# Five engine queues of an attention and MLP kernel, issued in another written order

## The chip, the cores and the metric

The kernel runs on one core of a Trainium2 chip. The metric is the device time of one execution in microseconds (us); before the change three runs took 714.17, 713.13 and 709.47 us, a median of 713.13.

A core has a matrix engine (TensorE, PE in the profile), a vector engine (DVE), a scalar engine (ScalarE, ACT), GpSimd (POOL), and a sync engine (SP) that here only issues DMAs. Each engine takes its instructions in the order of its own queue and waits at the head of the queue until what that instruction needs is there.

## The reference

Inputs are q, k, v of 4 batches, 8 heads, 768 positions and 64 dimensions in fp32, and the weights of a gated MLP (512 to 1536 to 512) with an RMSNorm gain.

```python
k_sum = k.reshape(B, H, nb, 32, D).max(axis=3)     # 24 block keys
v_sum = v.reshape(B, H, nb, 32, D).mean(axis=3)
scores_l = scale * q @ k.T, kept where |i - j| < 16
scores_s = scale * q @ k_sum.T + log(32)
a = softmax of both together
out = a @ concat(v, v_sum)
x = out, 3072 tokens of 512
xn = x / rms(x) * rms_g
(silu(xn @ w_gate) * (xn @ w_val)) @ w_out
```

## The kernel before, in words

The tokens are cut into 24 units of 128 (batch 0 is units 0 to 5, batch 3 units 18 to 23), and the units into groups for the MLP of 384, 128, 256 and then six times 384 tokens (`GROUPS`, groups 0 to 8). A product in full precision is made of fp16 high and low halves, three matmuls to a product.

The work is a list of some 760 steps (`PLAN`), each a call of one function. The names that the change and the prediction use:

- `su_*` (L889 to L1078): units 0 to 5 in fp32, loaded at the start; `su_vsum` (L961) sums v by blocks on PE, `su_v2` (L1002) and `su_v` (L991) load rows of v.
- `load_gv`, `decode_gv`, `split_gv` (L550 to L590) and `load_o`, `decode_o`, `scale_o`, `row_o`, `conv_o` (L557 to L650): bring the weights in, scale them and split them into halves. `row_o` takes sums of squares on ACT (L627), `scale_o` makes scales of them, and `conv_o` writes the scaled output weights (L649, L650).
- `sum_load`, `sum_fold`, `sum_scale` (L657 to L710): load k and v of batches 1 to 3 by pieces into two buffers (`hn`), fold each to block sums on ACT (L676) and POOL (L682), and scale a half batch with a small matmul (L699).
- `load_unit`, `load_k`, `prep_k`, `prep_q`, `fill_k`, `prep_v` (L744 to L820): load a unit's q, k and v, scale and split them. `prep_k` and `prep_q` each turn their tile with a transposing DMA on SP (L729, L796: `kT`, `qT`).
- `scores u g` (L822): matmuls L834 out of `kT` and `qT`, two to each unit; `expo u g` (L844): exponentials on ACT (L849), the split by ACT and POOL (L431, L436), and a transposing DMA on SP (L858: `eT`); `attend u` (L861): matmuls L875 out of `eT`, and the division on DVE (L879 to L881), which also frees the attention's PSUM banks.
- `norm_a`, `norm_b` (L1079, L1090): RMSNorm and a transposing DMA on SP (L1111: `xT`).
- `gate_val grp f T` (L1245, matmuls L1258) and `project grp f T tok0` (L1282, matmuls L1292): the MLP of a group by 12 slices f of 128 hidden columns.
- `make_t`, `make_s`, `seven`, `swish` (L1141 to L1243): for groups 5 to 8 the gate and value products in a seven-product scheme, matmuls L1190.

What an engine does first is not left to a scheduler. `ORDER` (L149) holds for each of the five queues (PE, Activation, DVE, Pool, SP) a permutation of that queue's instructions, numbered as the steps of `PLAN` make them: each entry is a jump from the last number, and "xN" a run of N consecutive numbers. `in_order` (L334) decodes it and ties every instruction to the one before it on its queue:

```python
for run in runs.split():
    jump, _, count = run.partition("x")
    n += int(jump)
    seq += range(n, n + int(count or 1))
    n = seq[-1] + 1
for a, b in zip(seq, seq[1:]):
    tc.add_manual_dep(traced[e][b], traced[e][a].name, after, reason="order")
```

Of the kernel before, what the change touches and what calls it, by code (L numbers as in the profile page):

```python
# [1339 lines left out]
```

## Time and profile before

| what | us |
|---|---|
| three runs | 714.17, 713.13, 709.47 |
| median | 713.13 |
| the profiled execution | 715.84 |
| its span, first to last instruction | 713.8 |
| PE busy in the span | 676.3 |
| DVE busy | 546.8 |
| ACT busy | 497.0 |
| POOL busy | 221.4 |

Some 2.0 us of the profiled execution lie outside its span. The mean granted clock of TensorE was 0.988 of full speed. "Busy" counts the time in which an engine runs an instruction; the page's matmul times overlap each other, so idle time of PE is what its busy time leaves of a stretch.

### The profile page before, as it was taken

How to read it: one execution, taken by the hardware profiler on the slowest of the kernel's cores; microseconds unless marked ns; L12 is line 12 of the kernel's file. 1: busy time of each engine (PE TensorE's matmuls, PEld its weight loads, DVE VectorE, ACT ScalarE, POOL GpSimd, SP SyncE). 2: the span in 40 equal slices, each digit the busy share in tenths (PEclk: the TensorE clock that was granted, in tenths of full speed). 3: DMA queues.
4: the chain of work that ended last, by engine and by line, in shares of the span. 5: the costliest groups of instructions: out<-in, count | busy, mean ns of one | idle time of the engine just before them, and what ended most of it. 6: DMA issues, size and time to landing. Idle time of an engine off the chain costs nothing.

```text
span 713.8 us, 16151 instructions
## 1 busy us (share of the span) xinstructions
PE 676.3 (95%) x5854; PEld 480.1 (67%) x5854; DVE 546.8 (77%) x1599; ACT 497.0 (70%) x1095; POOL 221.4 (31%) x321
## 2 busy tenths in 40 slices
PE   6898999977999999999999999999999999999997
PEld 4586767963457755565565555787877688878873
DVE  3698988958779957677989789998888778675443
ACT  3597877678997768756876776877788668744433
POOL 5473332550234244512132444232133213310000
PEclk9999999998999999999999999999999999999999
DMA  9999644634688768778569857193759563320001
GB/s 190 290 330 250 207 156 126 125 86 82 119 171 160 154 150 154 153 141 138 134 137 175 134 124 152 29 165 69 146 116 148 116 87 74 65 53 31 16 30 45
DMA packets 243860, 93.33 MB, mean 131 GB/s; under 512 B 227716, under 2 KB 227716, under 8 KB 243780
## 3 DMA queue, kind: packets, MB, share of 16 engines
q1 hardware_dynamic: 239172, 84.78, 57.1%
q10 hardware_dynamic: 3456, 6.29, 2.4%
q0 software_dynamic: 1152, 1.22, 0.8%
q8 instruction: 46, 0.75, 0.5%
q14 instruction: 34, 0.28, 0.1%
HBM read 50.45 MB, written 6.59 MB: 80 GB/s over the span
## 4 chain that ended last, share of the span: by engine, by line
PE 54%; DVE 13%; ACT 11%; DMA 10%; issue 5%; SPq 4%; POOL 2%; ACTq 0%; POOLq 0%; DVEq 0%
PE acc L1292 14%; PE gv L1190 14%; PE gv L1258 14%; PE acc L1258 4%; DMA eT<-ee 3%; SPq L745 3%; DMA qT<-qs 2%; PE att L875 2%; PE att L834 2%; DVE sm L838 2%; ACT sm L849 1%; DMA hn<-in_v_dram 1%; ACT junk L627 1%; DMA xT<-xs 1%; PE att L1026 1%
## 5 line engine op out<-in xcount | busy, mean ns | idle before, releaser
L1292 PE MATMUL acc<-wo,hhl 128*128 128x512 f16 x864 | 232.0, 382 | 4.2 <-ACT wo L649 2.8
L1258 PE MATMUL gv<-xT,w_gv 128*128 128x384 f16 (+2 forms) x1296 | 219.3, 305 | 3.3 <-DVE vv L820 0.9
L1258 PEld LDWEIGHTS <-w_gv 128*128 128x128 f16 x1584 | 141.4, 99 | 75.2 <-issue 5.6
L1292 PEld LDWEIGHTS <-hhl 128*128 128x128 f16 x864 | 81.6, 98 | 66.6 <-issue 5.1
L436 POOL TENSOR_TENSOR ee<-sm,ee 128x256 f16<-128x256 f32 (+1 forms) x72 | 68.0, 961 | 163.6 <-ACT ee L431 149.4
L1190 PEld LDWEIGHTS <-w_gv 128*128 128x128 f16 x1008 | 86.6, 98 | 9.1 <-issue 0.4
L849 ACT ACTIVATE sm<-sm,mx,c 128x192 f32<-128x192 f32 x144 | 70.6, 538 | 1.5
L1190 PE MATMUL gv<-S,w_gv 128*128 128x192 f16 x504 | 63.8, 246 | 0.1
L838 DVE CUSTOM_DVE_ANT_0 sm<-att,mask 128x192 f32<-128x192 f32 x144 | 44.3, 351 | 10.7 <-POOL ee L436 8.0
L1190 PE MATMUL gv<-xT,w_gv 128*128 128x192 f16 x504 | 52.1, 246 | 0.0
L1190 PEld LDWEIGHTS <-wo 128*128 128x128 f16 x540 | 47.0, 98 | 7.1 <-issue 1.9
L1190 PE MATMUL gv<-xT,wo 128*128 128x192 f16 x360 | 48.9, 246 | 1.2 <-DVE xT L1178 0.8
L875 PEld LDWEIGHTS <-eT 128*128 128x128 f16 x720 | 36.2, 97 | 18.2 <-DMA eT<-ee 4.4
L875 PE MATMUL att<-vv,eT 128*128 128x65 f16 x720 | 44.1, 193 | 4.2 <-DMA eT<-ee 3.0
L834 PE MATMUL att<-kT,qT 128*128 128x192 f16 x288 | 41.9, 246 | 4.2 <-DMA qT<-qs 3.0
L436 POOL TENSOR_TENSOR xs<-x,xs 128x512 f16<-128x512 f32 x21 | 25.2, 1202 | 53.4 <-ACT xs L431 48.2
L1258 PE MATMUL acc<-xT,w_gv 128*128 128x384 f16 (+1 forms) x288 | 40.6, 273 | 0.0
L676 ACT ACTIVATE junk<-hn 96x512 uint8<-96x512 f32 x48 | 30.0, 625 | 12.7 <-DMA hn<-in_v_dram 7.4
L1267 ACT ACTIVATE th<-gv,gains 128x384 f32<-128x384 f32 (+1 forms) x42 | 22.8, 544 | 22.9 <-PE gv L1258 15.6
L431 ACT CAST ee<-sm 128x512 f16<-128x512 f32 (+1 forms) x72 | 34.7, 507 | 5.8 <-DMA eT<-ee 4.8
L682 POOL TENSOR_TENSOR hn<-hn 96x512 f32<-96x512 f32 x18 | 22.9, 1271 | 45.6 <-DMA hn<-in_v_dram 27.3
L834 PEld LDWEIGHTS <-qT 128*128 128x128 f16 x288 | 25.8, 98 | 16.6 <-DMA qT<-qs 4.6
(308 smaller groups left out, 1347.2 us busy)
## 6 DMA issues: line engine op xcount, KB each, us to landing
wo<-in_moe_w_gate_dram SPq DMA_DIRECT2D x6, 1024.0 KB
wo<-in_moe_w_val_dram SPq DMA_DIRECT2D x6, 1024.0 KB
wo<-in_moe_w_out_dram SPq DMA_DIRECT2D x6, 1024.0 KB
out_dram<-ob ACTq DMA_DIRECT2D x23, 256.0 KB
hn<-in_k_dram SPq DMA_DIRECT2D x24, 192.0 KB
hn<-in_v_dram SPq DMA_DIRECT2D x24, 192.0 KB
qr_l<-in_q_dram SPq DMA_DIRECT2D x15, 256.0 KB
vr_l<-in_v_dram SPq DMA_DIRECT2D x15, 256.0 KB
```

The lines of the kernel that those rows point to most:

```text
L431: nc.scalar.copy(o, i)
L436: (nc.vector if ENG.get(op, "p") == "v" else nc.gpsimd).tensor_tensor(o, a, b, op=ALU.subtract)
L676: nc.scalar.activation(junk[0:96], y[:, o:o + DM], AF.Square, accum_out=d["ss"][:, j:j + 1])
L682: eng.tensor_tensor(x[:, 0:w], x[:, 0:w], y[:, 0:w], op=op)
L834: nc.tensor.matmul(pt[:, j * SC:(j + 1) * SC], lhsT=s["qT"][:, a * H + h, :], rhs=kT[:, h, :], start=(a == 0), stop=(a == 1))
L838: nc.vector.tensor_tensor_reduce(sm[:, i, :], pt[:, j * SC:(j + 1) * SC], mask, 1.0, NEG, op0=ALU.add, op1=ALU.max, accum_out=mx[:, i:i + 1])
L849: nc.scalar.activation(sm[:, i, :], sm[:, i, :], AF.Exp, scale=s["c"][:, 0:1], bias=mx[:, i:i + 1])
L875: nc.tensor.matmul(po[r][:, h // 2, 0:D + 1], lhsT=e, rhs=vv[:, 0:D + 1], start=(n == 0), stop=(n == len(pairs) - 1))
L1190: nc.tensor.matmul(bank[:, i * T2:(i + 1) * T2], lhsT=right(n, wi, c), rhs=left(xi, c), start=start, stop=(i == 1 and c == 1 and wi == 1), ...
L1258: nc.tensor.matmul(pt[:, 0:T], lhsT=w_gv[:, f - f % 2 + i, wi, c, f % 2, :], rhs=x[:, xi, c, 0:T], start=(n == 0), stop=(n == 3 * NC - 1))
L1267: nc.scalar.activation(th, pg[:, 0:T], AF.Tanh, scale=f_sc[:, f - f % 2:f - f % 2 + 1])
L1292: nc.tensor.matmul(accs[grp][j], lhsT=h[:, js], rhs=wo_hl[f // 2][:, wi, f % 2, :], start=(f == first and n == 0), stop=(f == (first - 1) ...
```

## The change

Only the five strings of `ORDER` are replaced. `PLAN`, the functions, the tiles, the buffers and the number of instructions on each queue (PE 5709, Activation 1003, DVE 1407, Pool 330, SP 382) stay, and each new string is a permutation of the same numbers. So nothing is computed otherwise, and every wait for data stays; what changes is what stands ahead of what on a queue. The first line of the PE and of the SP string, old and new (a leading - is the diff's mark):

```diff
 ORDER = dict(
     PE="""
-0x52 6x4 -10x6 4 1 -2 1 4x6 -10x4 34x3 -28x2 -4 -2 1 4x5 3 -4x3 16x4 1 -32 10 1 18x2 -20x2 -4 -12 14 4 -5x4 1 7 3x2 1
...
+0x22 36x2 -38x18 20 -21x8 13 -14x10 8x4 -7 -2 2 -2 13 4x2 -15x4 1 1 -4 1 27x3 -22 -7x2 5 20x2 1 -2 2x2 -23x2 -6x4 23
...
     SP="""
-1 -2 21 -20 -2 1 13 -14x2 13 -12 9 -5x2 -9 -2 4 -2 9 -8 -5 2 3 8x2 1 27 -27 -2 1x2 1 -11 -3 78 -45 -35 3 7 -3 11 -3 -8
...
+2 17 -21x2 20 -4 -17x2 10 -11x2 4 -4 7 -5 -6 1 4 -5 2 3x2 2 5 -4 7 2 -3 -6 2 -2 -8 2 12 -11 -5 33 -2 -15 3x2 -14 20 -13
...
```

Decoded, the order shows these moves (positions on a queue count from 0; "ahead" and "behind" are seen from the instruction named):

| queue | first instruction of | position | what changed sides |
|---|---|---|---|
| SP | `su_v 2` | 20 to 18 | behind now: 2 loads of `su_v2 0` |
| SP | `load_gv 4` | 25 to 34 | ahead now: 7 loads of `su_v2`, `load_gv 5`, `load_gv 6` |
| SP | `load_gv 11` | 54 to 58 | ahead now: `sum_load 1 0 0 2` and 6 loads of `su_v2`; behind now: 2 of `load_unit 6`, 1 of `su_v2 3` |
| ACT | `decode_gv 4`, its last pass | 49 to 50 | ahead now: a copy of `norm_b 0` |
| ACT | `sum_fold 1 1 1 1` | 141 to 139 | behind now: one pass each of `decode_o 10` and `gate_val 1 5`; `norm_a 5` stays ahead |
| ACT | `conv_o 0` | 170 to 168 | behind now: one pass each of `prep_q 6` and `gate_val 2 1` |
| DVE | `scale_o`, last pieces | | between them no longer: `prep_k 8` |
| PE | `gate_val 3 0` | 1738 to 1741 | ahead now: 3 matmuls of `project 2 10` |
| PE | `scores 10 0` | 1761 to 1762 | ahead now: the same 3; behind now: 2 of `gate_val 3 0` |
| SP | `expo 14 1` | 258 to 257 | behind now: the transposition of `norm_b 12` and a load of `load_unit 16`; ahead now: another load of `load_unit 16` |
| ACT | `expo 14 1` | 519 to 518 | behind now: copies of `make_t 4`, `make_t 5`, a pass of `gate_val 4 7` |
| POOL | `expo 14 1` | 233 to 231 | behind now: 2 DMA issues of `prep_v 14`, a pass of `norm_a 13` |
| PE | `scores 16 1`, second matmul | 2908 to 2974 | ahead now: 31 matmuls of `attend 15`, 24 of `gate_val 5 7`, 11 of `project 4 10` and `4 11` |
| DVE | `attend 15` | | five of its passes now in one run; `make_s 5 0` was between |
| PE | `scores 19 0` | 3697 to 3718 | ahead now: 21 matmuls of `seven 6 1` |
| PE | `scores 20 0` | 3962 to 3971 | ahead now: 7 matmuls of `seven 6 3`, 2 of `project 6 3` |
| PE | `attend 20` | 4200 to 4208 | ahead now: 8 matmuls of `seven 6 5` |
| PE | `scores 22 0` | 4452 to 4476 | ahead now: 24 matmuls of `seven 7 1` |

Everywhere else neighbours change places as well, mostly by a few positions; on SP, whose queue is the shortest, the moves reach farthest in time.

## Rows read from the trace of the kernel before

**Rows 1.** The page's part 1: busy us and share of each engine
```profile
PE 676.3 (95%) x5854; PEld 480.1 (67%) x5854; DVE 546.8 (77%) x1599; ACT 497.0 (70%) x1095; POOL 221.4 (31%) x321
```

**Rows 2.** Windows: length, busy of PE, PEld, DVE, ACT, POOL; clock, DMA share, GB/s
```profile
0.00:60.00 60.00, 49.08 (x370) 37.09 (x371) 41.02 (x145) 37.28 (x63) 34.75 (x82) 0.96 0.97 268
60.00:140.00 80.00, 79.97 (x698) 58.72 (x697) 69.61 (x186) 58.26 (x105) 28.03 (x39) 0.99 0.58 164
140.00:180.00 40.00, 31.17 (x258) 21.73 (x257) 28.07 (x94) 32.82 (x80) 12.68 (x19) 0.87 0.52 99
180.00:280.00 100.00, 96.66 (x761) 61.64 (x760) 78.37 (x252) 80.35 (x192) 33.55 (x45) 1.00 0.76 154
280.00:380.00 100.00, 99.71 (x731) 59.47 (x729) 78.61 (x238) 70.43 (x161) 33.19 (x44) 1.00 0.70 137
380.00:440.00 60.00, 55.06 (x391) 32.12 (x389) 52.80 (x144) 41.58 (x100) 23.19 (x26) 1.00 0.76 145
440.00:520.00 80.00, 78.79 (x811) 62.68 (x809) 71.45 (x209) 60.30 (x141) 20.90 (x26) 1.00 0.56 106
520.00:600.00 80.00, 76.18 (x808) 61.91 (x807) 63.10 (x194) 61.56 (x142) 22.98 (x32) 1.00 0.64 109
600.00:714.00 114.00, 109.64 (x1043) 84.74 (x1040) 63.72 (x144) 54.43 (x118) 12.11 (x14) 1.00 0.19 45
```

**Rows 3.** A window of 3.4 us at half clock, the same columns
```profile
164.10:167.50 3.40, 2.23 (x5) 0.66 (x5) 3.40 (x11) 3.35 (x9) 0.00 (x0) 0.51 0.40 75
```

**Rows 4.** Waits of PE: line, releaser, total us, times, longest us
```profile
PE att L699 <- ACT junk L676: 3.8, 1, 3.8
PE att L834 <- DMA qT<-qs: 3.0, 4, 1.1
PE att L875 <- DMA eT<-ee: 3.0, 2, 2.5
PE acc L1292 <- ACT wo L649: 2.8, 1, 2.8
PE att L576 <- ACT w_gv L570: 2.3, 1, 2.3
PE acc L968 <- DMA v1f<-in_v_dram: 2.0, 1, 2.0
...
PE att L834 <- DVE x L881: 1.2, 1, 1.2
...
PE att L875 <- DVE mx L838: 1.0, 1, 1.0
...
PE gv L1258 <- DVE th L1270: 0.4, 2, 0.2
```

**Rows 5.** Timeline of SP's queue at the start
```profile
17.42 4.51 SPq L745 DMA_DIRECT2D v2f<-in_v_dram  x1
```

**Rows 6.** Timeline of 142 to 165 us, ACT and DVE
```profile
142.94 0.63 ACT L1084 ACTIVATE junk<-x 128x512 uint8<-128x512 f32 x1 [1.14 <-DVE x L1073]
...
143.70 0.63 ACT L676 ACTIVATE junk<-hn 96x512 uint8<-96x512 f32 x1
...
163.05 0.74 DVE L724 SCALAR_TENSOR_TENSOR khl<-kr,kv_s,khl 128x512 f16<-128x512 f32 x1
...
164.15 0.46 ACT L1267 ACTIVATE th<-gv,gains 128x256 f32<-128x256 f32 x1
```

**Rows 7.** Timeline of SP's queue before the matmuls of attend 14
```profile
383.99 2.32 SPq L1111 DMA_TRANSPOSE xT<-xs  x1
...
387.37 2.32 SPq L858 DMA_TRANSPOSE eT<-ee  x1
```

**Rows 8.** Timeline of SP's queue before scores 20 0
```profile
525.91 3.26 SPq L796 DMA_TRANSPOSE qT<-qs  x1
```

**Rows 9.** Chain of waits: two pieces, start us, us, what, with matmuls
```profile
452.12 1.08 PE acc L1292 x5
...
507.50 1.98 PE gv L1190 x24
```

More of the change, by code (lines that the diff above doesn't have):

```diff
@@ new lines @@
+88x9 121x3 2 -3 -125x5 120 1 -123x3 120 -121 122 -77 2 -3 2x2 12 55 2x2 -4 -74 -49x2 63 -14 2x3 8 -65x2 49 13 -64x2
+62x3 -10 9x13 43 -3 2x3 -5 5 -2 1x5 4 -5 4 -5x3 2x8 -68 -31 30x3 -30 3 -4x2 27x20 44 7 -8x2 1 -2 1x2 -51 50 -51x3 138
+-188 190 -83x21 -32 1 38 -10x3 -32 -3 40 -39 38x2 -40 39 -38 37 47 -5x2 29 -75x9 39x2 -32 -57 82 -27 -11x2 9x2 -11x7
+-59 3 -4 30x2 -5 33x20 -49 -5x2 87 -4 3 -4 3 -4 3x3 -34x6 6 -7 6 -7 6x3 -9 8 -9 8 -9x2 7x2 55 3 -60x3 53 3x3 -6 86
+-132x4 11 -12x5 36 86 -117 116 2 -3x2 5x2 -6x4 5 -138x2 6 -7x2 14 -10 128 -129 -7 6 122 27 -24x2 -6x2 -107 -4 -23 6x2
@@ new lines @@
+-7 64x2 -60 69 -11 10 -11 10 85 -165 67x4 7x2 -9x4 5x6 -77 76 -81 3 -4 4x2 91x5 7 -8 7 -8x2 6x2 -8x4 4 46 -47x2 40
+-41x2 39 3x2 -5 4 -46 45 -159 -7 158 -157 166 -6 5 -93 86x2 4x3 -53 -4 48x2 10 -58x2 50x2 4 -57 56 -63 62 -7 6 -7 -99 1
+96 5 4 -5x2 -62x2 60x2 -56x2 55x4 -112 44 7x2 -9 8 -9 8 -9 168 -216 -5 6 -3 214x2 1 -221 55 -9x2 171 -217 213 2 -216x2
+-6 219 -167x3 164 -215x2 -3 101 -106 53x2 3 -4x2 161 2 -3 2 -3 2x2 -220 53 45 10x2 -12 11x3 -14x3 11x2 -13 12x2 -14x5
+9x3 -67x3 -4 -4 70x4 8 -9x4 5 -6x3 3 -4 3x9 54 -4 3 -4 -5 7 -4 -5x2 -51x2 10x2 -12x4 234 2 -3 -236x2 6 -7 6 -7x3 4x8
@@ new lines @@
+82x2 2x3 -5x2 3 -90x2 10 -11x4 7 -8 7x3 -10x3 7 200 -129x3 1 -77x3 -11x2 9x2 190 -74x2 -119 71x2 117 -73 77 109x3
+-284x2 10 -11 163 5 -125 235 -272 -11 10x2 -12x2 10 261x3 -264x3 -14x6 273 -266x2 264 -265x4 18 4x9 3x2 31 -37x3 34 5
+-6x2 4x2 -6 5 -6 5 5 -12 5x2 4 -5 4 -5x2 3x6 -57x3 54x3 3 -4 -58x4 57 -4x2 2x3 -61x3 -46x2 1x2 -6 2 2 43 -4 5 93x3 1
+-98 -4 3 -8 56 11 -12x4 8x2 -10x3 7x2 -9 8 -9 8 -9x2 7 -76 2 6x2 64x4 26x5 -8x2 -4 3 12x3 -10x3 7x4 -11 10x2 -12 11 -12
+-105 104 -105 -7 155 4 -5 4 -5x3 -160 203 -43 2 -160 198 -86x2 41x2 5x3 -7 -160 123 41 -173 172 -97x2 -8 7 86x3 10
@@ new lines @@
+-15 129x2 2 -3 2 -139 138 -4 5x4 -6x2 5 -120 119 -3 -146 -5 6x2 146x3 -6 -106 -43 26 18x10 92x2 -154 59x2 95 1 -2 5x3
+-7x3 4 -5 5x3 -4 3x2 -131 30 -13 12x8 -20 19x3 -22x10 -73 42 53x7 -19x12 7x5 -70x2 68x7 5x2 -7x4 3 -4 3x9 -87 -6 2 2
+151x5 7 -8x5 3 -4x2 2 -38x2 1 -7 6 -7 3 -4 5 32 8 -9x3 6x3 -9x3 6 -7x2 -41 8 36x9 -45x7 38x5 5 -6x2 4 -5 4 -5x2 3x18
+3x5 -8x2 6x2 -8 7x5 -98 2x3 -5 114 11 -12x2 10 -11 10 -11x4 7 -8x4 4 -131 -5x2 133x4 3 -4 3x2 -5 4 -5 4 -44 -4 5 40x4 3
+-4x3 1x2 45x3 -98 97 -49x2 7 -8x2 6 38x4 -42 -8x2 6 -7x3 -58 -8x2 67 7 -8 38x3 2 -107 106 -4x2 2 2x2 -4 3x2 -5 4x2 4
@@ new lines @@
+-8x3 5 -6x2 4x8 8 2 5 -143 142x2 9 -10x2 8 -9x4 5x2 -7x2 -14 -6 5 17x2 -7 6x6 -29 -3 2 2 92 -69x4 8 -9x8 1x4 43x2 2
+-3x2 1x3 -51 6x4 -10x3 7 -8 7 -8x2 6x6 50x3 2 -3 2 -3 2x2 1x2 -3 2x7 1 -2 1 3 -4 3 -4x2 2x2 1x5 -6 5x5 -55 2 -39x3 9
+-10x2 8x2 -10x2 8x3 -11 10 -11x2 9x2 -11x2 9 11 -12x2 15 -4x2 -4 5x2 2 2x2 -4 -4 6 -7 2 78 11x2 -13x3 10x2 -12x3 9 -43
+-10 2 2x2 -7 2 47 -40 -4 31x2 9x2 -11x2 -32 -4 -4 -4 49x2 -55 20 -7 -6 11 21 10x2 -41 1 4 -11 5 -3 2 3 2 2 -3 -4x2 4 -3
+39 -56 55x11 -24 59 -60x6 29x2 -31x2 29 -30x3 27x3 19 -87 66 -19x2 17x3 -20 19x2 -21x9 33x12 -33x12 6 -4 29x7 -19 18
@@ new lines @@
+-20x5 5x2 -57 -63 118x3 5x5 -69x5 -13 -51 -4 3 -4x2 2 60 11x4 -83 82 -16x2 14x2 -16 15x2 -17x3 14 -15x3 12x2 -14x2 58
+-7x2 1 3x2 36 11x2 -13x4 9 -10 9x3 -12 -48x2 -4 60 -12x2 -42 2 -3 -5x2 5 -3 2 -7 42 9x2 -11 10x3 -13 -33 -7 6 -5 4 -8
+2x2 -4 12 -4 -4 3 2 -7 52x12 -24 -35 -7 2 37 34x2 -36x2 34x3 -37 36 -37x2 35 -36x5 31x4 -80 2 76 -24x11 25x2 -27 26x10
+-24x12 24x11 -23 22 -23x11 24x9 -21x4 17 -18x4 14 -15x3 12 -13 -135 -3 -4x2 2 1 145 11 -12x2 10x11 -21x9 30x23 1 -2
+1x21 2x2 -4x2 2x14 -251 250x4 4x2 -6 5 -6 5 -6x2 4x8 -102x2 118x8 4 -5x4 1x12 -142 -2 1 140x2 9x2 -11 10 -11 10 -11
@@ L270 @@
--44 40 2 3x2 -3 -3 4 1x2 -3 6 -5 4 -5x3
+0x5 12 -13x2 2 2 -2 1 1 -9 6 13 -21 1 5 6 -6 15 -6 -9 -3x2 1 12 2 -15 1 -2 10 -10 11 -7 -3 -2 6 -6 7x2 5 -6 1 7 4 -15
+1x2 1 4 4 -10x3 8 2 -5 -6 6 2 -9 10x2 5 -20 10 13 -6 -14 2 6 -2 15 -19x2 10 -9 2x2 10 9 -17 -5x2 13 -10 39 -26 -15 6 -4
+5x3 -12 7 -5 -8 16 -10 10 25 -24 -2 -4 4 25 -25 27 -34 8 -6 21 -14 -8 62 -59 2 -8 22 -7 -10x2 14 -15 -8 26 -6 -15x2 30
+-31 -13 29 -4 -24 9 4 8 9 -19 -6 21 7 -7 22 -12 11 -10 -29 4x6 3x2 1x2 1x3 86 -86 7 -7x2 83 -52 -31 -8 7 10 -2 19 -5
@@ new lines @@
+1 -2 -6 25 -28 24x2 -23 19 -16 19 -35 1 -2 -16 33 12 -47x2 27x2 9 -38 12 15 1 13 -14 5 -40 49 15 -4 -11 -25 35 -2 -14
+16 -7 -15 18 -16 -29 10 -2 19 -18 21 -24 24 7 -10 -3 12 -16x2 26x2 -10 -5 -71 67 -22 -24 46 1 1x2 12 -18 12 1 3 2 -17
+-2 -25 34 -10x2 14 -3 -13 10 3 -7 9x4 -7 7 4 4 -30 17 1 9 -33 22 -10 9 8 -7 15x2 2 -23 22 1 -90 90 -2 -18 11 -19 8 -2
+-2 38 -18 13x2 -24 -5 12 -3 16 -33 34 -2 -37 -2 3 -3 38 -3 5 -4 4 -31 6 -3x2 -3 21 2 -21 -2 1x2 -37 51 3 -33 -40 81 7
+-39 19 3 -4 9 -30 19x2 8 7 -16 8x2 3 -7 13 -20 12 -16 -41 62 -7 4 -22 1 -19 39x2 2 -12x2 8 -2 3 -2 -7 -5 -5 -6 20 14
@@ new lines @@
+1x3 -8 7 -18 -13 8 20x3 -14 5 -34 40x2 -37 36x3 1x2 2 -3 2x2 -8 24 -17 1 -8 10 -8 1 1x2 3 -4 1 1 5 -5x4 2 -8 14 -6 -3 4
+2 -3 6 -11x2 -4 7x4 3 -2 -2 4x2 -4x2 2 1 -2 1 1 1 -2 -3 3x3 3x2 -5 1 -2 3 2 -2 8 -2 -7 1 -2 -5 5x2 4 -2 5 -10 4x4 5 -2
+2 -2 -5 6 -2 -8 8 -8 11x2 -6x3 8 -9 2x3 5 -5 -2 2 3 -2 -3 3x2 3x2 -5 1 -2 3 4 -4 1 -4 1 9 -8 5 -3 9 -6 -2 -8 1 -2 8 -7
+11 -6x2 4x3 -5 -2 6 -2 -12 12x4 5 -4x3 1 -6 11 -2 -6 6 3 -11 7x2 -9x3 -12 19 -2 3 -2 -2 7x2 -3 -3 -2 -11 11 4 -2 2x2
+1x2 -15 11 4 -2 -2 3x2 2 -2 -2 -13 15x3 4x2 -5 -2 2 -14 5 5 4 -2 4 -2 -2 -2 3 2 -2 -2 2x2 2 -2 -2 3x2 -3 2x2
@@ L330 @@
+-20 42 -43 31 10 -20 -10 17 13 -36 9 18 -36 22 -4 23 -3 -18 17 1 -8 1 -17 14 8 -3 -28 1 8 2 -5 4 16 -3 -22 18 -17 18
+-29 31 -23 32 -10 1 1x2 -7 7 17 -16 6 -22x2 3 26 -21 17 2 -18 17 -20 28 -27 5 -5 -2 6 -2 16 -20 24 -32 -11 19x2 -7 -13
+35x2 3 -13 10 -14 2 -5 -2 7 -13 36 -20 -9 -4 18 -13 25 -14 -3 -5x2 1 4 -2 10 2 -20 26 -13 13x2 2 -3 -22 -4x2 2x2 -4 3 4
+9 5x2 -4 -11 -3 4 -2 -4 1 2 10 -2 1 1 -2 1
 """,
```

289 lines of the change are left out of this document (121 added, 168 removed).

## The prediction

> **What bounds the kernel now.** Part 1 of the page comes first: PE is busy 676.3 us of 713.8, far ahead of DVE with 546.8 and ACT with 497.0 [rows 1]. An order of issue can't shorten a matmul, so at most PE's idle 37.5 us are to be had, and what PE loses while its clock is halved. Where they lie is in the windows by stretch [rows 2]. Length less PE busy gives 10.9 us idle before 60, 0.0 to 140, 8.8 from 140 to 180, 3.3 to 280, 0.3 to 380, 4.9 to 440, 1.2 to 520, 3.8 to 600, and 4.4 after that, with the last output's way out among it. From 60 to 140 and from 280 to 380 nothing can be gained; there any wait that the new order makes is a loss in full. The granted clock stands at 1.00 from 180 on and falls below it in the first stretches; five windows of 3.4 us lie at 0.50, which is 1.2 of 2.4 GHz, behind a wait of PE each time but once, where one window follows another (one of the five is in [rows 3]). The waits of PE by what ended them [rows 4] then give each hole a name: an ACT pass (L676, 3.8 us; L649, 2.8; L570, 2.3), a first load (`v1f`, 2.0), turned queries (`qT`, 3.0 in four), turned exponentials (`eT`, 3.0 in two), and DVE's division (L881, 1.2) that frees a PSUM bank. I followed each releaser back in the timeline, and then read in the decoded order what stands ahead of it, and of the waiting matmul, on every queue.
>
> **The change part by part.** No instruction goes or comes; each term is a wait that shrinks or grows, in the profiled execution's time (715.84 us; span 713.8 and 2.0 around it).
>
> Start, 0 to 60. The wait for `v1f` (2.0) ends with a load that stood behind a 4.51 us hold of SP by a load of `su_v2` [rows 4, 5]. In the new order two loads of `su_v2 0` go behind it, but the big loads of k, q, v and the weights stay ahead, and SP's lanes stay full. I take 0.5 off, between 0 and the whole 2.0. The wait for L570 (2.3) is for the last pass of `decode_gv 4`, now behind one more ACT copy; a pass of this width is 0.63 us by the pass in [rows 6]. The su_expo passes that also moved ahead of `decode_gv 4`'s first pass only fill ACT's earlier time. I add 0.2, between 0 and 0.6 us. Net -0.3.
>
> 140 to 180. The longest wait (3.8) is for `sum_fold 1 1 1 3`, at the end of a chain in which a fold frees a buffer, SP loads into it, and the next fold follows. The fold before it on ACT, at 143.70, is now ahead of `decode_o 10`. Yet `norm_a 5` still stands between, and it had itself waited until 142.94 for DVE's x [rows 6]. DVE gives that x no earlier in the new order, so the chain doesn't start sooner: 0, between -1.0 and +1.5. The wait for `conv_o 0` (2.8) shrinks: ACT no longer does a 0.46 us pass of `gate_val 2 1` ahead of it, and DVE no longer does the 0.74 us pass of `prep_k 8` between the scales [rows 6]. Both lie on one path and are shared with other pieces that moved in: -0.8, between 0 and -1.2. The half-clock windows stay, since the waits before them stay long.
>
> 180 to 280. Three matmuls of `project 2 10` go ahead of `gate_val 3 0` and `scores 10 0`; five such take 1.08 us [rows 9], so three take 0.65. They cover most of one `qT` wait.
>
> `attend 14`, 2.5 us of the two `eT` waits [rows 4]. Its transposition was issued at 387.37 behind that of `norm_b 12`, which held SP 2.32 us from 383.99 [rows 7]. In the new order `norm_b 12` goes behind, and ACT and POOL make the exponentials with three and three instructions fewer ahead. The matmuls of `attend 14` move by 3 places. I take -2.4, between -2.5 and 0. `norm_b 12`'s own transposition feeds group 5, whose matmuls start after 400, so that its delay of 2.32 us lies beside work.
>
> `scores 16 1`, 1.2 us for DVE's L881 [rows 4]: 66 matmuls go ahead, and the passes of `attend 15` on DVE run together. -1.2, between -1.2 and 0.
>
> The `qT` waits of `scores 19 0`, `20 0` and `22 0`, with that of `scores 10 0` four waits of 3.0 together [rows 4]. A seven-product matmul takes 1.98 / 24 = 0.083 us, a `project` matmul 1.08 / 5 = 0.216 [rows 9]. Ahead go 21 x 0.083 = 1.7, 7 x 0.083 + 2 x 0.216 = 1.0, and 24 x 0.083 = 2.0. Each covers its wait (the longest is 1.1) or all but a tenth of it; I take -2.7 for all four, between -3.0 and -0.5. `attend 20` gets 8 x 0.083 = 0.7 ahead of its 1.0: -0.7.
>
> The sum of what shrinks: 0.3 + 0.8 + 2.4 + 1.2 + 2.7 + 0.7 = 8.1. Against that stands what comes late next. Some of the moved passes must be late for something, and where a wait closes PE reaches the next one sooner. The smallest waits in the list are of 0.2 us, the named ones of 1.0 and more [rows 4]. For eight closed waits I take a quarter of a microsecond each, near the smallest, 2.0 in all, between 0 and 8. Net 8.1 - 2.0 = 6.1 less: 709.7 on the profiled execution's scale, and 713.13 - 6.1 = 707.0 on that of the median, 2.7 below it.
>
> The Trainium skill (DMA: Bandwidth & Descriptors, section "Issuing engines are not separate DMA queues") says that transfers all end on the same 16 DMA engines and interleave there. By that rule the transposition of `norm_b 12`, though issued later, would still share the engines with that of `attend 14` and hold back its landing. The DMA share of 0.76 from 380 to 440 [rows 2] leaves room for either reading. If the rule took the whole term of `attend 14`, the sum would be -3.7 in place of -6.1, or 709.4.
>
> **The rivals.**
>
> (a) More than forecast, faster by over 1% (713.13 / 100 = 7.1 us, about what a measurement of this kernel can tell from no change). Here the startup or the stretch from 140 to 180 closes too. If the `v1f` wait went in whole (1.5 more than I take) and the one for L676 by 2 us, and if thereby two half-clock windows ended, each worth up to half its 3.4 us, the gain would be 6.1 + 1.5 + 2.0 + 3.4 = 13.0: 700. For it: these stretches hold more than half of PE's idle time [rows 2]. Against it: the chain through `norm_a 5` and the order of the big loads, as read above.
>
> (b) Nothing to measure: each closed wait opens at the next producer. Late in the kernel DVE and ACT feed PE through one long chain per unit, and DVE is busy 71.5 of 80 us from 440 to 520 [rows 2]. PE then arrives early and waits for `attend` instead. Only `attend 14` and half of the rest remain, and new waits of 4 us come on top: -2.4 - 2.9 + 4 = -1.3, 712.
>
> (c) Slower: SP. A transposition of queries holds SP 3.26 us [rows 8], and one load whose buffer isn't free has held it 4.51 [rows 5]. In the new order loads of `load_unit` go ahead of transpositions in many places. If one of them isn't ready, `qT` or `eT` of the unit lands later by such a turn. Priced in the place where the waits already stand, units 18 to 23: a turn of 3.26 less the 1.0 that the matmuls ahead cover is 2.26, in six units 13.6. With the gains of `qT`, `attend 20` and `attend 14` gone (5.8), the time would be 707.0 + 5.8 + 13.6 = 726.4. It decides against the change by over 1% from four such units on (707.0 + 5.8 + 4 x 2.26 = 721.8). For it: SP's moves reach farthest. Against it: in the rows SP's holds late in the kernel are its transpositions themselves, whose number stays.
>
> **How the numbers follow.** The forecast, between 703 and 711, has 0.50, (a) 0.25, (b) 0.15 and (c) 0.10. The forecast's own case lies across the 1% bound of 706.0: its lower part, some 0.16, counts as faster. Faster: 0.25 + 0.16 = 0.41; slower: 0.10; the rest, 0.49, within 1%. The range takes the forecast, (b), most of (a) and the milder half of (c): 698 to 717.
>
> **What would show it.** Right: `attend 14` waits under 0.5 us for `eT`; `qT` has at most one wait over 0.5; L881 is gone from the list of PE's waits; PE's idle time from 380 to 440 is 1 to 2 us and from 520 to 600 about 2; the 3.8 us for L676 stays within 1.5. Wrong: a new wait of over 1.5 us on an `eT` or `xT` between 280 and 600, SP held over 3.5 us by a load there, PE idle more than 2 us from 60 to 140 or 280 to 380, or a change in the number of half-clock windows.

## The result, and the profile after

| | before | after |
|---|---|---|
| median of 20 runs, us | 714.21 | 707.98 |
| lowest to highest | 709.04 to 717.98 | 702.01 to 712.85 |
| ratio, 95% interval | | 0.9914 [0.989, 0.9938] |
| profiled execution | 715.84 | 708.47 |
| its span | 713.8 | 706.6 |

The change makes the kernel 0.86% faster, 0.0086 x 714 = 6.1 us. The interval is worth 4.4 to 7.9 us. Single runs of one order lie up to 11 us apart, and that matters below: one trace of each order shows their difference plus the difference of two executions.

The windows of the trace after, with the columns of [rows 2] (length, busy of PE, PEld, DVE, ACT, POOL, clock, DMA share, GB/s):
```profile
...
60.00:140.00 80.00, 76.76 (x655) 55.68 (x654) 65.03 (x177) 54.02 (x97) 24.38 (x40) 0.99 0.58 164
140.00:180.00 40.00, 32.54 (x282) 24.09 (x280) 27.79 (x91) 34.18 (x84) 11.66 (x17) 0.87 0.51 110
...
280.00:380.00 100.00, 98.95 (x728) 59.12 (x726) 78.71 (x241) 68.94 (x158) 28.43 (x38) 1.00 0.68 135
380.00:440.00 60.00, 59.35 (x423) 35.18 (x421) 54.25 (x152) 46.92 (x110) 30.16 (x31) 1.00 0.72 151
...
520.00:600.00 80.00, 79.30 (x845) 65.02 (x843) 63.66 (x196) 62.02 (x142) 23.21 (x32) 1.00 0.61 117
```
Against [rows 2]: from 380 to 440 PE's idle time falls from 4.9 to 0.7 us, from 520 to 600 from 3.8 to 0.7. From 60 to 140, where PE had none, it now has 3.2, and from 280 to 380 1.1 in place of 0.3.

PE's waits in the trace after, columns as in [rows 4]:
```profile
PE gv L1258 <- DVE th L1270: 4.1, 5, 2.7
PE att L699 <- ACT junk L676: 3.3, 1, 3.3
PE att L576 <- ACT w_gv L570: 3.3, 2, 3.0
...
PE gv L1258 <- DMA xT<-xs: 2.2, 1, 2.2
...
PE att L834 <- DMA qT<-qs: 1.0, 3, 0.4
PE att L875 <- DMA eT<-ee: 1.0, 2, 0.6
```
`qT` is down from 3.0 to 1.0 and has no wait above 0.4; `eT` from 3.0 to 1.0, none at `attend 14`; L676 stays at 3.3; DVE's L881, ACT's L649 and the load of `v1f` are out of the list. The waits at `attend 14`, for `qT`, for L881 and for L676 were named as signs that the forecast is right; PE's idle times after 380 were named too, and went below what was named (0.7 each, for 1 to 2 and about 2). Of the signs against, two are there. One is PE's idle time from 60 to 140. The other tells nothing: SP stands 6.8 us before a load of `sum_load 3 1 1 2`, but in the old order it stood 7.3 us before the same one. The half-clock windows are five, as before. In place of the old waits stand DVE's L1270 (4.1, of it 2.7 in one) and one `xT` of 2.2.

To compare executions stretch by stretch, I count what PE loses: the time that a stretch takes less the sum of its matmuls' issue intervals at full clock (512 columns 0.2155 us, 384 0.162, 192 0.082, and so for the other shapes, read from runs of matmuls without a wait; 645.9 us over the kernel). It holds waits and half clock alike. The last column ends with the last matmul, some 4 us before the span does. Cuts lie at equal amounts of work done, named here by their time in us in the first trace of the old order. The rows with an e are the experiments below.

| lost by PE, us | 0-85 | 85-142 | 142-193 | 193-272 | 272-378 | 378-455 | 455-end |
|---|---|---|---|---|---|---|---|
| old, first trace | 22.0 | 3.9 | 15.6 | 4.2 | 1.4 | 6.6 | 9.2 |
| old, again (e11) | 19.8 | 3.6 | 14.4 | 4.1 | 2.1 | 4.5 | 8.4 |
| new, first trace | 21.1 | 7.5 | 13.1 | 4.8 | 1.7 | 1.5 | 6.0 |
| new, again (e9) | 20.1 | 6.0 | 13.8 | 4.0 | 2.0 | 1.6 | 6.8 |
| old, then new from 372 (e1) | 20.2 | 4.6 | 15.0 | 3.5 | 3.1 | 1.9 | 7.0 |
| new, then old from 373 (e2) | 20.0 | 4.2 | 14.2 | 6.4 | 2.0 | 4.0 | 7.0 |
| new to 92, old, new from 372 (e3) | 22.8 | 4.1 | 15.2 | 3.9 | 2.5 | 2.5 | 5.7 |
| old, some late moves (e5) | 20.0 | 4.2 | 14.4 | 4.7 | 1.7 | 5.6 | 6.5 |
| new, an SP pair back (e4) | 20.9 | 4.3 | 12.9 | 3.8 | 1.7 | 1.5 | 6.0 |
| e4 with DVE moves (e6) | 19.3 | 4.2 | 12.1 | 3.5 | 1.3 | 1.5 | 6.4 |
| e4 with ACT moves (e7) | 20.3 | 4.4 | 11.5 | 5.5 | 1.7 | 1.5 | 6.1 |
| e4 with both (e8) | 21.2 | 4.3 | 10.3 | 3.5 | 1.5 | 1.5 | 6.4 |
| e8 again (e10) | 19.9 | 4.2 | 10.4 | 3.9 | 1.2 | 1.6 | 6.0 |

### The profile page after: what moved, and what is told of

It is laid out like the page before. It is cut to its first block, busy times and chain, and to the rows that moved or that the text cites. A ratio compares the mean times of both kernels' runs of the same rounds, so it can differ in the third digit from the quotient of the medians.

```text
span 706.6 us, 16113 instructions
## 1 busy us (share of the span) xinstructions
PE 676.8 (96%) x5854; PEld 482.1 (68%) x5854; DVE 540.8 (77%) x1599; ACT 497.3 (70%) x1095; POOL 221.4 (31%) x321
## 4 chain that ended last, share of the span: by engine, by line
PE 64%; DMA 12%; DVE 7%; ACT 6%; SPq 5%; issue 4%; POOL 2%; POOLq 0%; ACTq 0%; DVEq 0%
PE acc L1292 20%; PE gv L1190 17%; PE gv L1258 17%; DMA qT<-qs 4%; SPq L745 3%; PE att L834 3%; PE acc L1258 2%; PE att L875 2%; DMA eT<-ee 2%; DMA wo<-in_moe_w_val_dram 1%; DMA wo<-in_moe_w_gate_dram 1%; ACT junk L627 1%; SPq L554 1%; DMA hn<-in_k_dram 1%; POOL ee L436 1%
## 5 line engine op out<-in xcount | busy, mean ns | idle before, releaser
L436 POOL TENSOR_TENSOR ee<-sm,ee 128x256 f16<-128x256 f32 (+1 forms) x72 | 70.5, 991 | 154.7 <-ACT ee L431 132.0
L1190 PEld LDWEIGHTS <-w_gv 128*128 128x128 f16 x1008 | 87.3, 98 | 12.1 <-issue 1.5
L1190 PE MATMUL gv<-S,w_gv 128*128 128x192 f16 x504 | 65.7, 246 | 0.0
L1190 PE MATMUL gv<-xT,w_gv 128*128 128x192 f16 x504 | 54.6, 246 | 0.6 <-DVE R L1224 0.5
L1258 PE MATMUL acc<-xT,w_gv 128*128 128x384 f16 (+1 forms) x288 | 43.0, 272 | 0.0
L875 PE MATMUL att<-vv,eT 128*128 128x65 f16 x720 | 42.0, 193 | 1.0 <-DMA eT<-ee 1.0
L1087 POOL TENSOR_TENSOR x_r<-x_r,consts 128x1 f32<-128x1 f32 x24 | 21.1, 879 | 53.5 <-DVE x_r L1086 44.4
L676 ACT ACTIVATE junk<-hn 96x512 uint8<-96x512 f32 x48 | 29.9, 624 | 10.2 <-DMA hn<-in_k_dram 5.2
L431 ACT CAST ee<-sm 128x256 f16<-128x256 f32 (+1 forms) x72 | 34.9, 507 | 1.9 <-DMA eT<-ee 1.2
L1268 DVE SCALAR_TENSOR_TENSOR th<-th,gv 128x384 f32<-128x384 f32 (+1 forms) x42 | 21.5, 511 | 18.9 <-ACT th L1267 18.9
```

Of the source, the lines that this page charges most:

```text
L431: nc.scalar.copy(o, i)
L436: (nc.vector if ENG.get(op, "p") == "v" else nc.gpsimd).tensor_tensor(o, a, b, op=ALU.subtract)
L676: nc.scalar.activation(junk[0:96], y[:, o:o + DM], AF.Square, accum_out=d["ss"][:, j:j + 1])
L875: nc.tensor.matmul(po[r][:, h // 2, 0:D + 1], lhsT=e, rhs=vv[:, 0:D + 1], start=(n == 0), stop=(n == len(pairs) - 1))
L1190: nc.tensor.matmul(bank[:, i * T2:(i + 1) * T2], lhsT=right(n, wi, c), rhs=left(xi, c), start=start, stop=(i == 1 and c == 1 and wi == 1), ...
L1258: nc.tensor.matmul(pt[:, 0:T], lhsT=w_gv[:, f - f % 2 + i, wi, c, f % 2, :], rhs=x[:, xi, c, 0:T], start=(n == 0), stop=(n == 3 * NC - 1))
```

## The experiments

A queue's order is given decoded in the diffs, since the numbers of the strings say nothing. The run with the number n here has the label that begins with en. The strings' length shifts the lines of these kernels, by 1 or 2 in e1 to e4 and e6 (L1270 is L1271 or L1272), by -5 in e7, e8 and e10 (L1265).

**e1 to e3: which half carries it.** Each queue is cut where an execution stood at one moment; what had been issued by then keeps one order, the rest takes the other.
```diff
 e1, each queue
-old order
+old order up to 372 us of its trace, then the rest in the new order
 e2, each queue
-old order
+new order up to 373 us of its trace, then the rest in the old order
 e3, each queue
-old order
+new order up to 92 us, then the old up to 372, then the new
```


> Old order on all five queues until 372 us of the old trace (just ahead of the passes for attend 14), the new order for all that is left. Theory A, the gain is a sum of local waits and the stretches in which PE never waits keep them apart: PE's work done at a given time lies 1.6 us later in the new order than in the old at this cut and 6.9 us earlier at the end, so the late part alone should be worth 1.6 + 6.9 = 8.5: ratio to before 0.988, waits of attend 14, scores 16 1 and scores 20 0 under 0.3 us. Theory B, the late gains need what the early part moved (loads and preparations brought forward): half of it at most, ratio 0.994 or above. Theory C, the gain comes from the first 100 us: ratio 0.998 to 1.002.

> The other half: the new order until 373 us of the new trace, the old order for all that is left. Theory A: 1.6 us slower than before, ratio 1.002, and the old late waits come back (attend 14 about 2.5 us, scores 20 0 about 1.1). Theory B: between, 0.995 to 0.998. Theory C: 0.991.

> The new order until 92 us of the new trace, the old order until 372 us of the old one, then the new order. Theory A: the startup's gain (0.9 at that point) and the late part (8.5) add up without the loss between them: 9.4 less, ratio 0.987, and the wait for gate_val 1 0 (2.2 us in the new order) is gone. Theory B: the gain is that of the whole change or less, 0.991 or above, with new waits at the seams. Theory C: 0.991.

Measured: e1 0.9938 [0.9898, 0.9977], e2 0.9979 [0.9951, 1.0008], e3 0.9915 [0.9885, 0.9946]. Theory C falls. The late part alone brings 4.4 us, the early part 1.5 with an interval that includes no change; together 5.9, near the 6.1 of the whole. So the halves add, but the ratios alone don't decide for theory A: all three that it gave lie outside the intervals (its sizes were wrong by 4 us in e1 and 3 in e2), and those of theory B lie inside. What speaks for A is the trace of e1, whose early part is in the old order (its lines are 1 higher):
```profile
PE att L876 <- DMA eT<-ee: 0.9, 2, 0.7
...
PE att L835 <- DMA qT<-qs: 0.6, 2, 0.4
PE att L835 <- DVE x L882: 0.5, 1, 0.5
```
None of these is a wait that A named: the longest are at `attend 18`, `scores 10 0` and `scores 14 1`. From 378 on PE lost 8.9 us in e1, against 12.9 and 15.8 in the old order and 7.5 and 8.4 in the new. So the late waits close without the early moves. The table also shows why A's sizes were wrong: they were taken from one pair of traces, in which the first trace of the old order had lost some 2 us more at the start than its others, and whose stretch from 85 to 142 held a wait that e2, with the same order there, did not have (7.5 against 4.2). e1 and e3 also pay at the seam (3.1 and 2.5 from 272 to 378, where the others have 1.2 to 2.1).

**e4: the new `xT` wait.** In the trace after, SP's timeline and PE's wait:
```profile
114.88 0.31 SPq L693 DMA_DIRECT2D sum<-hn  x1
...
118.10 0.31 SPq L666 DMA_DIRECT2D hn<-in_v_dram  x1
118.46 1.34 SPq L1111 DMA_TRANSPOSE xT<-xs  x1
...
124.57 0.23 PE L1258 MATMUL gv<-xT,w_gv 128*128 128x128 f16 x1 [2.15 <-DMA xT<-xs]
```
SP issued a store of sums at 114.88, then nothing until 118.10: the load behind it goes into the buffer that the store reads, and the store had to land. The transposition of `norm_b 3`, which was ready, stood behind that load. In the old order it stood ahead.
```diff
 SP, decoded
   sum_fold 1 0 1 3
-  sum_load 1 1 0 1
   norm_b 3
+  sum_load 1 1 0 1
   load_ks 1
```


> The whole change, with one pair on SP's queue turned back: the transposition of norm_b 3 ahead of sum_load 1 1 0 1, as in the old order. In the new order that transposition was issued at 118.46, behind a load that SP held until 118.10 for its buffer, while the issue before had ended at 115.19. Theory A (the new 2.2 us wait of gate_val 1 0 for xT is head of line blocking on SP): the transposition is issued at about 115.2, the wait falls under 0.3, the time by about 2 us, ratio to before 0.988 or 0.989. Rival (the wait is the landing of the transposition itself among other transfers, or PE waits for another producer next): the wait stays over 1.5 or moves, ratio 0.991.

The trace of e4:
```profile
114.65 0.31 SPq L694 DMA_DIRECT2D sum<-hn  x1
115.07 1.34 SPq L1112 DMA_TRANSPOSE xT<-xs  x1
...
117.71 0.32 SPq L667 DMA_DIRECT2D hn<-in_v_dram  x1
```
The transposition goes at 115.07, the load still waits until 117.71, and PE doesn't wait at `gate_val 1 0`. The ratio is 0.9894 [0.985, 0.9939], below the 0.9914 of the change, but the intervals overlap, so the times don't tell theory A (0.988 or 0.989) from the rival (0.991). What settles it is the table's second column: the new order lost 7.5, 6.0 and 4.2 us from 85 to 142 in three executions, and with the pair turned back 4.2 to 4.4 in all five (e4, e6, e7, e8, e10). So the new order exposed PE to the time that one store takes to land, 1.9 to 3.2 us, and mostly, not always, paid for it.

**e5: the late waits, by PE's and SP's queue alone.**
```diff
 PE, decoded (the old order)
+  21 matmuls of seven 6 1
   scores 19 0, first matmul
+  7 matmuls of seven 6 3, 2 of project 6 3
   scores 20 0, first matmul
+  8 matmuls of seven 6 5
   attend 20, first matmul
+  24 matmuls of seven 7 1
   scores 22 0, first matmul
 SP, decoded (the old order)
+  expo 14 1
   norm_b 12
   load_unit 16
-  expo 14 1
```


> The old order with two things alone from the new one: on PE the matmuls put ahead of the first matmul of scores 19 0 (21), scores 20 0 (9), attend 20 (8) and scores 22 0 (24), and on SP the transposition of expo 14 1 ahead of that of norm_b 12. Theory A (each wait is local, and covering it on PE's queue alone is enough): the four waits of 0.6, 1.1, 1.0 and 0.7 fall under 0.3 each, about 2.9 us less. At attend 14 the POOL pass of its exponentials ended at 386.2 and the transposition was issued at 387.4, so SP alone gives 1.0 of its 2.5 us and the other 1.5 need ACT and POOL. Together 3.9: ratio 0.9945. Rival D (PE only reaches the next late producer sooner): the named waits go, but attend 19, seven 7 0 and others grow by as much, ratio 0.998 or above.

Measured: 0.9962 [0.993, 0.9994], or 2.7 us. The waits of its trace:
```profile
PE att L834 <- DVE x L881: 2.3, 1, 2.3
...
PE att L875 <- DMA eT<-ee: 2.1, 2, 1.2
...
PE gv L1190 <- DVE xT L1178: 1.1, 1, 1.1
...
PE att L834 <- DMA qT<-qs: 0.6, 1, 0.6
```
The three `qT` waits at `scores 19 0`, `20 0` and `22 0` are gone (the 0.6 left is at `scores 10 0`), so PE's queue alone covers them; the one at `attend 20` fell from 1.0 to 0.3. Part comes back as in rival D: the `eT` wait of `attend 19` is the 1.2, where the first trace had 0.5, and L1178 (`seven 7 0`) has 1.1, where it had 0.6. The whole change has neither; that this comes of its moves of what makes those two was not tried. `scores 16 1`, not treated here, waits 2.3 for L881 where it had 1.2. That isn't PE coming sooner: L881 stands on DVE behind a pass of `make_s 5 0`, here in e5 and in a second trace of the old order (e11):
```profile
424.26 2.78 DVE L1174 TENSOR_TENSOR R<-R 128x192 f32<-128x192 f32 x1
```
```profile
423.29 1.74 DVE L1174 TENSOR_TENSOR R<-R 128x192 f32<-128x192 f32 x1
```
The other passes of this line take 0.35 us. What stretches this one isn't shown; POOL worked beside it in both. In the new order the passes of `attend 15` no longer stand behind it.

At `attend 14` the wait is gone too, where I gave SP's queue 1.0 of its 2.5 us. SP in e5, behind POOL's passes of the exponentials:
```profile
382.46 1.79 POOL L436 TENSOR_TENSOR ee<-sm,ee 128x512 f16<-128x512 f32 x2 [0.82 <-POOL kr_l L713]
384.27 1.44 SPq L858 DMA_TRANSPOSE eT<-ee  x1
385.77 1.85 SPq L1111 DMA_TRANSPOSE xT<-xs  x1
```
The same place in the old order, in e11, in e2 (its lines are 1 higher) and in the first trace:
```profile
380.90 2.38 SPq L1111 DMA_TRANSPOSE xT<-xs  x1
...
381.43 1.79 POOL L436 TENSOR_TENSOR ee<-sm,ee 128x512 f16<-128x512 f32 x2 [0.83 <-POOL kr_l L713]
383.42 0.48 DVE L817 SCALAR_TENSOR_TENSOR vv<-v2r_l,kv_s,vv 64x256 f16<-64x256 f32 x1
383.93 0.32 SPq L745 DMA_DIRECT2D v2r_l<-in_v_dram  x1
384.35 1.63 SPq L858 DMA_TRANSPOSE eT<-ee  x1
...
388.71 0.33 PE L875 MATMUL att<-vv,eT 128*128 128x65 f16 x5 [0.31 <-DMA eT<-ee]
```
```profile
384.12 1.79 POOL L437 TENSOR_TENSOR ee<-sm,ee 128x512 f16<-128x512 f32 x2 [0.77 <-POOL kr_l L714]
...
387.04 1.97 SPq L859 DMA_TRANSPOSE eT<-ee  x1
...
391.98 0.33 PE L876 MATMUL att<-vv,eT 128*128 128x65 f16 x5 [0.88 <-DMA eT<-ee]
```
```profile
384.45 1.78 POOL L436 TENSOR_TENSOR ee<-sm,ee 128x512 f16<-128x512 f32 x2 [0.82 <-POOL kr_l L713]
...
393.93 0.24 PE L875 MATMUL att<-vv,eT 128*128 128x65 f16 x2 [2.51 <-DMA eT<-ee]
```
In all three SP issued the transposition 1.1 us after POOL's last pass. The transposition of `norm_b 12` had let SP go within 0.1 us of that pass; what held SP was the load of `load_unit 16` between the two, which waited for a DVE pass (L817). In e5 the transposition went at once, so SP's queue is worth those 1.1 us, near the 1.0 expected. The rest is landing: from the issue of the transposition to PE's matmul it took 6.6 us in the first trace, 4.9 in e2 and 4.4 in e11, while PE began to wait 5.2 us after POOL's last pass in each. So the old order waited 2.5, 0.9 and 0.3 with nothing else different at this place, and in e5, with a landing of some 4.8, the 1.1 were enough. What ACT's or POOL's moves bring was not tried.

**e6, e7 and e8: what the new order still leaves.** In the trace after, DVE ahead of the wait of 2.7 us:
```profile
166.86 0.41 DVE L1268 SCALAR_TENSOR_TENSOR th<-th,gv 128x256 f32<-128x256 f32 x1
...
167.31 0.47 DVE L1270 SCALAR_TENSOR_TENSOR th<-th,scales,gv 128x256 f32<-128x256 f32 x1
...
167.84 0.27 PE L1258 MATMUL gv<-xT,w_gv 128*128 128x256 f16 x1 [2.74 <-DVE th L1270]
```
The matmul wants a PSUM bank that this L1270 (`gate_val 2 0`) frees, and that pass stood behind `scale_o` and three of `prep_q 6`, these behind the row of `row_o` passes on ACT. At 359.34 DVE has the like:
```profile
359.34 1.78 DVE L1157 TENSOR_TENSOR w_gv<-S,w_gv 128x256 f16<-128x256 f32 x1
...
361.11 0.54 DVE L1268 SCALAR_TENSOR_TENSOR th<-th,gv 128x384 f32<-128x384 f32 x1
...
361.69 0.97 PE L1258 MATMUL gv<-xT,w_gv 128*128 128x384 f16 x5 [1.05 <-DVE th L1268]
```
```diff
 DVE, decoded (e6 and e8, from e4)
+  scale_h, last pass; gate_val 2 0, two passes
   prep_q 6, three passes
-  scale_h, last pass; gate_val 2 0, two passes
-  prep_k 8
   conv_o 0, two passes
+  prep_k 8
   ...
+  gate_val 4 4, two passes
   make_t 2
-  gate_val 4 4, two passes
   ...
+  seven 5 1
   swish 5 0 1
-  seven 5 1
   ...
+  seven 6 5
   swish 6 4 1
-  seven 6 5
 ACT, decoded (e7 and e8, from e4; the two steps move in PLAN alike)
+  row_o 0, two passes
   norm_a 5; sum_fold 1 1 1 1; gate_val 1 5; decode_o 10
+  row_o 1, two passes
   sum_fold 1 1 1 2
   ...
-  row_o 0, row_o 1
   row_o 2 to 5
```


> The order of the run with the SP pair turned back, and on DVE four passes moved ahead: the two of gate_val 2 0 ahead of three of prep_q 6 (with the last pass of scale_h, which they read), prep_k 8 behind both of conv_o 0; the two of gate_val 4 4 ahead of a 1.78 us pass of make_t 2; one of seven 5 1 and one of seven 6 5 ahead of one of swish. Theory A: the waits of PE that the new order made (gate_val 2 2: 2.9, gate_val 4 5: 1.2, seven 5 1: 0.5, seven 6 5: 0.8) were DVE passes standing behind others that nobody waited for; they fall to about 1.8, 0.1, 0.1 and 0.3, together 3.1 us: ratio to before 0.985. Rival D: the waits move to the matmul behind (project 0 0 for conv_o, the next slices), ratio 0.988 or above.

> The order of the run with the SP pair turned back, and on ACT the four passes of row_o 0 and row_o 1 brought into two gaps, ahead of norm_a 5 (where ACT waited 1.5 us for DVE) and behind decode_o 10 (where it waited 1.8 us for a load). In the plan the two steps move with them, ahead of norm_a 5 and of sum_fold 1 1 1 2. Theory E (from 152 to 168 us PE waits on ACT: twelve row_o passes of 0.755 us, then scale_o, then conv_o): the chain ends 3.0 us sooner, the wait for scale_o (1.5) goes and those of gate_val 2 2 and project 0 0 (2.9 and 1.0) shrink by 1.5 together: 3.0 less, ratio to before 0.985. Rival F (what bounds there is PE itself at 1.2 GHz, or DVE's passes behind scale_o): under 1 us, 0.988 or above. The wait of sum_scale 1 1 (3.4) stays by both.

> The two runs before together. Theories A and E: the terms add, but both shrink gate_val 2 2, which counts once (about 1 us): 3.1 + 3.0 - 1.0 = 5.1 less than with the SP pair alone, ratio to before 0.982 and below the change itself (0.991). Rivals D and F: 0.987 or above.

Measured: e6 0.989 [0.9859, 0.9922], e7 0.9868 [0.984, 0.9895], e8 0.9871 [0.9843, 0.9898]. By these times e6 and e8 came out where rivals D and F had put them, and e7 between E and F. From 142 to 193 PE lost 12.9 us in e4, 12.1 in e6, 11.5 in e7 and 10.3 in e8. So there the two add: 0.8 + 1.4 = 2.2 against 2.6. But each is well below what was expected. In e6 PE's loss at `gate_val 2 2` fell from 2.9 to 1.6, but `project 0 0` got a new one of 1.0, for `conv_o`, and `scores 6 0` one of 0.9, since `prep_q 6` now comes later; those of `gate_val 4 5` and `seven 5 1` went, and `gate_val 4 6`, `scores 17 1` and `scores 21 0` took 0.5 each. From 272 on e6 lost 9.2 us, as much as e4: rival D for most of the sum. In e7 the wait for `scale_o` went, but `gate_val 2 2` kept its length:
```profile
PE gv L1253 <- DVE th L1265: 4.2, 4, 2.8
PE att L694 <- ACT junk L671: 3.3, 1, 3.3
```
The 3.0 us that ACT saved were paid out as 1.4: theory E has its mechanism, rival F (DVE behind `scale_o`) half of its price. From 193 to 272 this trace lost 1.7 more than e4's, at `scores 9 0` and `scores 10 0`, so that it doesn't show by itself that e7 is faster; the runs do. For e6 to e8 the interval of one doesn't exclude the next. The stretch from 142 to 193 puts them in order, but e6 and e7 have one trace each, and the three executions of the new order lie 1.1 apart there (13.1 to 14.2).

**e9, e10 and e11: again, side by side.** e9 is the change, e10 is e8, e11 the old order, all unaltered and on one chip.

> The change itself once more, on the same chip as the next run. Two questions. First, which waits belong to the order and which to one execution: theory G (the waits at attend 14, scores 16 1, 19 0, 20 0 and 22 0 belong to the old order; the one of 2.3 us at gate_val 1 0 belongs to the new order only where the store ahead of it lands late; the one for v1f at the start belongs to no order) says 0.3 or less at each of the first five, anything from 0 to 2.5 at gate_val 1 0, and under 0.5 for v1f. Rival: gate_val 1 0 waits 2 us or more again, as a fixed price of the new order. Second, its ratio: 0.991.

> The change with the SP pair turned back, the DVE passes and the row_o passes moved, again, beside the change on one chip: 0.987 against its 0.991, a difference of 0.4% or some 3 us, if the sum of local terms holds; within 0.1% of it if they were chance.

> The old order once more, for one trace. Theory G: attend 14 waits 1 to 2.9 us, scores 16 1 some 1.3, scores 20 0 some 1.2 again; the wait for v1f (2.1 in the first trace) is under 0.5, as in the two mixed orders that begin as this one. Rival (the first trace of the old order was a slow one in its late part too): two of the three late waits are under 0.4.

Measured: e9 0.992 [0.9888, 0.9953], e10 0.9844 [0.9799, 0.9888] (medians 706.99 and 701.29 us); e11, one run, 709.72. So e10 lies 0.8% below e9, twice what was expected. The version with the pair turned back and the moves on DVE and ACT beats both kernels: the old order by 1.6% here and 1.3% in e8, the change by 5.7 us between the medians here and 0.4% between e8 and the first comparison. Its intervals only just touch or overlap those of the change. The waits of e10:
```profile
PE att L694 <- ACT junk L671: 3.4, 1, 3.4
...
PE att L829 <- DMA qT<-qs: 2.6, 4, 1.2
PE gv L1253 <- DVE th L1265: 2.2, 3, 1.4
```
The waits for L1265, which is L1270 of the change, are down from 4.1 to 2.2; the largest wait left is the sum fold's. `qT` is back at 2.6, more than the change had, the longest at `scores 10 0`. Its granted clock from 140 to 180 is 0.91 against 0.87 before and after, so that less time passes at half clock there:
```profile
140.00:180.00 40.00, 33.44 (x274) 22.73 (x271) 29.74 (x96) 36.72 (x86) 12.23 (x20) 0.91 0.60 116
```

Theory G came out in half. In e9 the five late waits are gone again, `gate_val 1 0` has none, yet the stretch lost 6.0: the wait had moved on to `gate_val 1 2`, 1.5 us for a DVE pass behind three of `decode_o` and, ahead of these, one of `split_ks 1`, which waited for `load_ks 1`, the load next behind that transposition on SP. In e11 `scores 16 1` and `20 0` waited 1.2 and 1.0, as expected, but `attend 14` less than 1, and `v1f` 1.5 where I expected under 0.5. The waits of e11:
```profile
PE att L834 <- DMA qT<-qs: 1.6, 3, 1.0
PE acc L968 <- DMA v1f<-in_v_dram: 1.5, 1, 1.5
PE att L834 <- DVE x L881: 1.2, 1, 1.2
PE att L875 <- DMA eT<-ee: 1.1, 2, 0.8
```
`v1f` is late in two of four executions that begin in the old order (2.0, 1.5, and in e1 and e5 0.4 or less) and under 0.4 in all that begin in the new one, but what the start loses is alike (19.8 to 22.0 against 19.3 to 22.8): PE then loses more at `split_gv 4` and `5` (2.5 in the old, 3.3 to 3.8 in the new). So the start gains nothing that these runs can show.

## Why the prediction was right

The forecast was 6.1 us less, and 6.1 were measured. The mechanism was right, a sum of local waits of which the late ones close and a new one opens; that the sum agrees to a tenth is luck, as its terms show. They are, by PE's loss in the table (means of the executions with one order in that stretch, those across a seam left out):

- *Start, -0.3.* Measured none: 20.5 against 20.6 us. A wait that ends with a landing was taken for one of the order, and what the new order adds at `split_gv 4` and `5`, 0.8 to 1.3, was taken as 0.2.
- *60 to 140, nothing to gain, any new wait a full loss.* Right, and it happened: 4.1 in the old order, 5.9 in the new (7.5, 6.0, 4.2). It is the 2.0 that I set aside for new waits, though as one of 2 us, not eight of a quarter. The mechanism is that of rival (c), a load on SP that isn't ready ahead of a transposition that is; it struck once and early, where (c) had put it six times and late.
- *140 to 180, -0.8.* 14.9 to 13.7, or -1.2. The reading that `norm_a 5` holds the fold's chain was right: L676 still waits 3.3 of 3.8. `project 0 0` lost its wait for `conv_o` (2.8), but most of that went to DVE's L1270. The gain is about the forecast's by another path: `project 0 8` also lost its 0.9, which I had not counted.
- *180 to 280, a part of the `qT` term, 0.4 to 0.7.* Not so: 4.1 before, 5.1 after. `gate_val 3 0` and `project 2 7` lost their waits, but `scores 8 1`, `gate_val 2 4`, `attend 8` and `gate_val 2 7` now cost some 0.5 each, and `scores 10 0` kept its own: PE lost 0.5 to 0.9 there in the five executions with the old order, 0.3 to 2.4 in the eight with the new one. The three matmuls put ahead don't cover it.
- *`attend 14` -2.4 and `scores 16 1` -1.2.* From 378 to 455 the loss fell from 5.0 to 1.9 (first, e9, e1 and e3), so -3.2 for the -3.6. In detail `attend 14` was over-sized (2.5, 0.9 and 0.3 us in three executions of the old order), and the reading of what held SP was wrong: not the transposition of `norm_b 12`, but the load behind it, and of the 2.5 the order's part on SP was 1.1. On the other side `gate_val 5 6`, which I had left as it was, lost a wait of 1.1 that two of the three had. `scores 16 1` was right (1.2 in all three): there L881 stood behind one pass of `make_s 5 0` that took 1.7 us.
- *`qT` and `attend 20`, -2.7 and -0.7.* The waits went, and the loss from 455 on fell from 8.2 to 6.4: -1.8. The size failed in two ways: `scores 19 0` and `22 0` waited less in other executions (0.7 and 0.8 us lost in the first trace, 0.2 and 0.4 in e11), and `seven 5 1` and `seven 6 5` got new waits of 1.0 and of 0.2 to 1.0.

The column means add to -3.2, about half of the 6.1 of the runs; with two to nine traces in a column, of executions that differ by some us, that is no contradiction, and no proof of each term either. What e1 and e2 show without them is that the part after 372 us brings most of it.

The Trainium skill (DMA: Bandwidth & Descriptors, section "Issuing engines are not separate DMA queues") gave 3.7 in place of 6.1, if the later transposition of `norm_b 12` had held back that of `attend 14` on the shared engines. In e5 the one was issued 1.5 us after the other, and the wait was gone. The other landed after some 4.8 us there and after 5.4 in the trace after, within the 4.4 to 6.6 of the old order, so the rule did not take the term; whether the sharing costs some tenths, these runs can't tell.

Rival (a) needed the start or the fold's chain to close, and neither did; e7 shortened what stands behind the fold by other moves, but the fold's own wait stayed at 3.3. Rival (b) holds for the moves on DVE (most of e6's terms came back), not for the change's own late part. Rival (c) holds at its one place, and the old order had the same thing at `attend 14`, which the new one took away. That the 4.51 us of [rows 5] were a buffer that wasn't free, as (c) says, the trace doesn't show: the landing that this load had to wait for came at 14.83, before its issue at 17.42.

## What to carry to other kernels

Where queues are written by hand, put nothing that waits for a landing ahead of something that is ready and that the busiest engine will want: the price isn't in every trace, so look for the place in the order, not for the wait in one profile. The old order had such a place (`attend 14`) and the new one has another (`gate_val 1 0`). Work that is ready anyway, put ahead of a matmul that waits, takes the wait away for nothing, if the engine's later producers don't depend on that matmul. A single trace names the waits well and sizes them badly: those that end with a DMA's landing vary by 2 us from one execution to the next. A wait that ends with an engine's pass can hold still (1.2 in three executions at `scores 16 1`), but need not: it was 2.3 there in e5, and the one before `scale_o` (L637) took 1.2 and 2.5 us in the two executions of the change.

## What was not expected of the hardware

The same store of sums, from issue to the load that waits for it, took 3.2 us in the trace after, 2.9 in e9 and 1.9 in e2, with the same order around it. The transposition at `attend 14` took 4.4 to 6.6 from its issue to PE's matmul in the old order, and a first load differed likewise (`v1f`, a wait of 2.0, 1.5 and under 0.4 us). The spread of some 10 us between runs of one kernel may have part of its source there; that isn't shown. It also goes with the granted clock: of 56 runs of the old order beside the experiments, the twelve with the lowest mean clock (0.980 to 0.983) have a median of 714.2 us, the seven with the highest (0.989 and 0.990) one of 709.5. Which of the two brings the other isn't shown either.
